# Context and output matmuls of an attention block as two 64-row tiles, ordered by a GpSimd relay

## The chip, the cores and the metric

One NeuronCore of one Trainium2 chip. The metric is the device time of the core in microseconds (us); lower is better. A ratio is the mean time of one kernel's runs over that of the other's of the same rounds, so it is not quite the ratio of the medians that are quoted.

## The reference

A layer norm, then two branches on the normalized rows: a sliding-window attention over a cache (32 heads of 192, the last 512 keys, 2048 query rows) and a SwiGLU feed-forward whose SiLU gates the attention output.

```
xn = layernorm(x)                                    # (1, 2048, 640)
q  = xn @ wq                                         # 32 heads of 192
s  = softmax(q k^T / sqrt(192)) v                    # last 512 keys of the cache
s  = s.reshape(2048, 32 * 192) @ wo                  # 640 columns
g  = silu((silu(xn @ w_gate) * (xn @ w_up)) @ w_down)
return x + s * g
```

## The kernel before

The kernel walks over 16 pairs of heads. A pair has two phases on TensorE. The first makes projections (`q_rows`) and scores for four blocks `b` of 512 rows; its matmuls use 64 of the array's 128 rows, two at a time (the "lo" and "hi" partitions). The second makes context (`pv`, N = 193) and output projection (`wo_tile`, N = 320); its matmuls use all 128 rows. The output lags the context by two blocks, since the context is transposed by a DMA in between. PSUM is two tags of two buffers each: `sc` (scores and output tiles) and `mm` (projections and context). Buffers of a tag are taken in turn.

```python
    def sc_tile():
        return psum.tile([P, 2, 512], f32, name="sc", tag="sc")     # bufs=2
    def mm_tile():
        return psum.tile([P, 2, 512], f32, name="mm", tag="mm")     # bufs=2
...
    def scores(i, kc):
        khat, qT, ks = pairs[i // NB]["khat"], qTs[i], slice(kc * P, (kc + 1) * P)
        sc = mm_tile() if i == NS - 1 and kc < 2 else sc_tile()
        for j in range(3):
            for h, r in enumerate((lo, hi)):
                nc.tensor.matmul(
                    sc[:, h, :], khat[r, j, ks], qT[r, j, :], start=(j == 0), stop=(j == 2)
                )
        p_t = ppool.tile([P, 2, 512], bf, name="p_t")
        nc.scalar.activation(p_t[:, :, :], sc[:, :, :], ACT.Exp, scale=scale)
...
    def pv(i, q2):
        ...
        acc = sc_tile() if alone and q2 and b < 2 else mm_tile()
        for k in range(2):
            qt = 2 * q2 + k
            for h in range(2):
                for kc in range(KC):
                    nc.tensor.matmul(
                        acc[:, k, h * 256 : h * 256 + Dh + 1],
                        Ps[i][kc][:, h, qt * P : (qt + 1) * P], V_p[:, kc, h, 0 : Dh + 1],
                        start=(kc == 0), stop=(kc == KC - 1),
                    )
        ...                      # reciprocal on VectorE, four scaled copies on ScalarE to O_b
        if pr == last or i == 0:
            ...                  # a transposing DMA for each half of the block
        elif pr < last and q2 == 1:
            nc.sync.dma_start_transpose(
                out=OT_b[:, :, :], in_=O_b[:, :, :, :].rearrange("p t h d -> p (t h d)")
            )
...
        for b in range(NB):
            i = pr * NB + b
            for q2 in range(2):
                pv(i, q2)
                if i >= 2:
                    wo_tile(i - 2, 2 * q2)
                    wo_tile(i - 2, 2 * q2 + 1)
```

The softmax here doesn't subtract the row's maximum and nothing guards it: scores larger than these inputs give would overflow.

Of the kernel before, what the change touches and what calls it, by code (L numbers as in the profile page):

```python
# [10 lines left out]
ALU = mybir.AluOpType  # L11
# [4 lines left out]
def kernel(  # L16
# [13 lines left out]
    nc = tc.nc  # L30
    P = nc.NUM_PARTITIONS
# [4 lines left out]
    _, Hkv, Sk, Dh = A_k_cache.shape  # L36
# [8 lines left out]
    NB = Sq // 512  # L45
    KC = W // P
# [4 lines left out]
    HD = D // 2  # L51
    scale = float(Dh) ** -0.5
    EPS = 1e-5
    bf = dt.bfloat16
    f32 = dt.float32
# [6 lines left out]
    kk, vv, wq, wo = A_k_cache[0], A_v_cache[0], A_wq, A_wo  # L62
# [8 lines left out]
    def sc_tile():  # L71
        return psum.tile([P, 2, 512], f32, name="sc", tag="sc")

    def mm_tile():
        return psum.tile([P, 2, 512], f32, name="mm", tag="mm")
# [5 lines left out]
    g2 = res.tile([P, T, D], bf, name="g2")  # L81
# [11 lines left out]
    V_p = consts.tile([P, KC, 2, Dh + 2], bf, name="V_p")  # L93


    pairs = {}
# [46 lines left out]
    def sum_k(pr, c):  # L143
        d = pairs[pr]
        nc.vector.reduce_sum(d["ssum"][:, c : c + 1], d["KT"][:, c, :], axis=AX.X)

    lo, hi = slice(0, 64), slice(64, 128)
# [17 lines left out]
    with ExitStack() as fctx:  # L165
# [154 lines left out]
        first = {f: [sc[:, s, :] for s in range(2)] for f, sc in ((0, sc_tile()), (1, sc_tile()))}  # L320
# [16 lines left out]
        banks = [(f, s) for f in range(3) for s in range(2)]  # L337
# [69 lines left out]
    opool = ctx.enter_context(tc.tile_pool(name="att_o", bufs=2))  # L407
    otpool = ctx.enter_context(tc.tile_pool(name="att_ot", bufs=3))
    smpool = ctx.enter_context(tc.tile_pool(name="att_sm", bufs=8))
    finp = ctx.enter_context(tc.tile_pool(name="fin", bufs=2))  # L410
    sacc = sapool.tile([P, T, D], f32, name="sacc")

    NS = NPAIR * NB
    last = NPAIR - 1
    Ps, OTs, Obs, xrs = {}, {}, {}, {}

# [3 lines left out]
    def q_rows(i, j):  # L420
        pr, b = divmod(i, NB)
        if j == 0:
            qTs[i] = qpool.tile([P, 3, 512], bf, name="qT")
        q_ps = mm_tile()
        for c in range(NC):
            for h, r in enumerate((lo, hi)):
                nc.tensor.matmul(  # L427
                    q_ps[:, h, :], pairs[pr]["wq"][r, c, j * P : (j + 1) * P], xnT[r, c, b * 512 : (b + 1) * 512],
                    start=(c == 0), stop=(c == NC - 1),
                )  # L430
        with nc.allow_low_precision(reason="a sum of two, rounded once, like a copy out of PSUM"):
            nc.vector.reduce_sum(  # L432
                qTs[i][:, j, :], q_ps[:, :, :].rearrange("p h n -> p n h"), axis=AX.X
# [6 lines that stand above are left out]
# [8 lines left out]
    def pv(i, q2):  # L448

        pr, b = divmod(i, NB)  # L450
        if q2 == 0:
            Obs[i] = opool.tile([P, 4, 2, Dh], bf, name="O_b")
            tag = "OT_l" if late(i) and pr < last else "OT_b"
            OTs[i] = otpool.tile([P, 12, P], bf, name=tag, tag=tag, bufs=2 if tag == "OT_l" else 3)
        O_b, OT_b = Obs[i], OTs[i]
        alone = i < 2 or (pr == last and 2 * b + q2 < 5)
        acc = sc_tile() if alone and q2 and b < 2 else mm_tile()
        r = smpool.tile([P, 2, 2, 1], f32, name="r")
        for k in range(2):
            qt = 2 * q2 + k  # L460
            for h in range(2):
                for kc in range(KC):
                    nc.tensor.matmul(  # L463
                        acc[:, k, h * 256 : h * 256 + Dh + 1],
                        Ps[i][kc][:, h, qt * P : (qt + 1) * P], V_p[:, kc, h, 0 : Dh + 1],
                        start=(kc == 0), stop=(kc == KC - 1),
                    )
        a_v = acc[:, :, :].rearrange("p k (h c) -> p k h c", h=2)
        nc.vector.reciprocal(r[:], a_v[:, :, :, Dh : Dh + 1])  # L469
        for k in range(2):  # L470
            qt = 2 * q2 + k
            a_k = a_v[:, k, :, :]
            if k == 0 and alone:
                nc.vector.tensor_tensor(  # L474
                    O_b[:, qt, :, :], a_k[:, :, 0:Dh], r[:, k, :, :].to_broadcast([P, 2, Dh]),
                    ALU.mult,
                )
                continue
            for h in range(2):
                nc.scalar.activation(  # L480
                    O_b[:, qt, h, :], a_k[:, h, 0:Dh], ACT.Copy, scale=r[:, k, h, :]
                )
        if pr == last or i == 0:
            nc.sync.dma_start_transpose(
                out=OT_b[:, 6 * q2 : 6 * q2 + 6, :],
                in_=O_b[:, 2 * q2 : 2 * q2 + 2, :, :].rearrange("p t h d -> p (t h d)"),
            )
        elif pr < last and q2 == 1:
            nc.sync.dma_start_transpose(
                out=OT_b[:, :, :], in_=O_b[:, :, :, :].rearrange("p t h d -> p (t h d)")  # L490
            )

    def load_xr(t):
        xrs[t] = finp.tile([P, D], bf, name="x_r", bufs=8)
        nc.sync.dma_start(out=xrs[t][:], in_=x2[t * P : (t + 1) * P, :])


    def late(i):
        return i // NB >= NPAIR - 2 and i % NB >= 2

    def wo_mm(ps, i, qt, n, first=True, end=True):
        for j in range(3):
            nc.tensor.matmul(  # L503
                ps, OTs[i][:, 3 * qt + j, :], pairs[i // NB]["wo"][:, j, n * HD : (n + 1) * HD],
                start=(first and j == 0), stop=(end and j == 2),
            )

    def wo_tile(i, qt):
        pr, b = divmod(i, NB)
        t = 4 * b + qt  # L510
        sc = sc_tile()
        for n in range(2):
            wo_mm(sc[:, n, 0:HD], i, qt, n)
        s_t = sacc[:, t, :].rearrange("p (n d) -> p n d", n=2)
        if pr == 0:
            nc.vector.tensor_copy(out=s_t, in_=sc[:, :, 0:HD])
        else:
            nc.vector.tensor_tensor(s_t, s_t, sc[:, :, 0:HD], ALU.add)  # L518

        if pr == last - 1 or late(i + NB):  # L520
            nc.gpsimd.tensor_tensor(sacc[:, t, :], sacc[:, t, :], g2[:, t, :], ALU.mult)  # L521
            if pr < last - 1:
                add_x(t)

    def add_x(t):
        nc.gpsimd.tensor_tensor(sacc[:, t, :], sacc[:, t, :], xrs[t][:], ALU.add)
# [29 lines left out]
    def store(left):  # L556
        while len(stores) > left:
            t, ob = stores.pop(0)
            nc.sync.dma_start(out=out2[t * P : (t + 1) * P, :], in_=ob[:])

    for pr in range(NPAIR):
        for b in range(NB):
            i = pr * NB + b
            for kc in range(KC):
                if kc < 3 and i + 1 < NS:
                    q_rows(i + 1, kc)
                scores(i, kc)
                if pr < last:
                    if b == 0:
                        transpose_k(pr + 1, kc)  # L570
                    elif b == 2 and kc < 3:
                        sum_k(pr + 1, kc)
                    elif b == 3:
                        centre_k(pr + 1, kc)
                        if kc == 3:
                            centre_k(pr + 1, 4)
            if b == 0:
                load_v(pr)
                if pr >= last - 1:
                    for t in range(8):  # L580
                        load_xr(t + 8 if pr < last else t)
                        if pr == last:
                            add_x(t)
        if pr == last:
            break
        for b in range(NB):
            i = pr * NB + b
            for q2 in range(2):
                pv(i, q2)
                if i >= 2:  # L590
                    wo_tile(i - 2, 2 * q2)
                    wo_tile(i - 2, 2 * q2 + 1)
            if b == 0 and pr + 2 < NPAIR:
                load_k(pr + 2)
            elif b == 1 and pr + 2 < NPAIR:
                load_wq(pr + 2)
            elif b == 2:
                load_wo(pr + 1)
    i = last * NB
    V, G = nc.vector, nc.gpsimd  # L600
    work = [(0, 0), (0, 1), (1, 0), (1, 1), (2, 0)]
    for b, q2 in work:
        pv(i + b, q2)
    for b, q2, more in ((0, 0, (2, 1)), (0, 1, (3, 0)), (1, 0, (3, 1)), (1, 1, None)):
        for k in range(2):
            wo_last(b, 2 * q2 + k, G)
        if more:
            pv(i + more[0], more[1])
    for b in (2, 3):
        for qt in range(4):  # L610
            store(0 if (b, qt) == (3, 3) else 3)
# [31 lines left out]
```

## Time and profile before

| | before |
|---|---|
| device time, median | 927.87 us (927.74 to 927.89, 4 runs) |
| profiled span | 925.9 us |
| TensorE busy | 918.9 us, 99% |
| one pair, start to start | 47.24 us: 23.42 projections and scores, 23.83 context and output |
| mode changes of TensorE in pairs 0-13 | 28, each 0.096 us over the normal spacing |

TensorE is the bound, so the total is read off its start times: what is late there is late at the end. The useful view is the order of time around the two borders of a pair, since the start of a group, less that of the group before, against the number of matmuls in it, shows what was lost between them. The lines are in the prediction.

### The profile page before, as it was taken

The numbers are of one execution on the slowest core, as the hardware profiler recorded it, in microseconds if no ns is written. First come the engines' busy times: TensorE is split into PE (matmuls) and PEld (weight loads), VectorE is DVE, ScalarE is ACT, GpSimd is POOL, SyncE is SP. The second block draws the span as 40 slices with busy tenths as digits, with TensorE's granted clock in tenths as the row PEclk, the third lists the DMA queues.
The fourth block names the chain that finished last, engine by engine and source line by source line (L and its number), as shares of the span: only waits on it lengthen the run. The fifth ranks groups of instructions, "written<-read, shape, count | busy, mean of one in ns | idle before, by whom it ended". The sixth has DMA issues, their size and how long they took to land. (4 is left out here: it accounts for less than half of the span.)

```text
span 925.9 us, 18772 instructions
## 1 busy us (share of the span) xinstructions
PE 918.9 (99%) x7997; PEld 578.0 (62%) x8013; DVE 576.6 (62%) x844; ACT 474.0 (51%) x847; POOL 68.0 (7%) x59
## 2 busy tenths in 40 slices
PE   9999999999999999999999999999999999999997
PEld 5455556574848474757575757565666666666665
DVE  6433331467676767676666667676767676767655
ACT  4222222556465656565555555555555565656561
POOL 0000000000000000000000000000000000002977
PEclk9999999999999999999999999999999999999999
DMA  9321510053525343343434252526262616162524
GB/s 296 74 53 35 114 35 1 1 93 71 101 63 92 73 85 79 76 88 70 94 68 96 59 106 55 109 49 116 40 124 35 129 35 125 37 132 75 142 50 140
DMA packets 241892, 76.73 MB, mean 83 GB/s; under 512 B 222736, under 2 KB 241808, under 8 KB 241808
## 3 DMA queue, kind: packets, MB, share of 16 engines
q1 hardware_dynamic: 240752, 74.71, 38.1%
q8 instruction: 63, 1.03, 0.5%
q10 hardware_dynamic: 1056, 0.82, 0.3%
q14 instruction: 21, 0.17, 0.1%
HBM read 39.45 MB, written 2.62 MB: 45 GB/s over the span
## 5 line engine op out<-in xcount | busy, mean ns | idle before, releaser
L445 ACT ACTIVATE p_t<-sc 128x1024 bf16<-128x1024 f32 x254 | 253.0, 1022 | 136.6 <-PE sc L441 136.6
L432 DVE TENSOR_REDUCE qT<-mm 128x512 bf16<-128x1024 f32 x189 | 231.3, 1224 | 104.0 <-PE mm L427 101.6
L480 ACT ACTIVATE O_b<-mm,r 128x192 bf16<-128x192 f32 x486 | 164.7, 421 | 176.5 <-DVE r L469 96.6
L427 PE MATMUL mm<-xnT,wq_p 64*128 64x512 bf16 x1890 | 235.1, 377 | 0.0
L503 PE MATMUL sc<-wo_p,OT_b 128*128 128x320 bf16 x1482 | 223.1, 299 | 0.0
L518 DVE TENSOR_TENSOR sacc<-sacc,sc 128x640 f32<-128x640 f32 x216 | 176.7, 821 | 60.9 <-PE sc L503 60.9
L441 PE MATMUL sc<-qT,khat 64*128 64x512 bf16 x1524 | 195.6, 376 | 0.0
L463 PE MATMUL mm<-V_p,p_t 128*128 128x193 bf16 x1984 | 186.0, 246 | 0.0
L463 PEld LDWEIGHTS <-p_t 128*128 128x128 bf16 x2048 | 173.0, 97 | 15.0 <-issue 7.0
L503 PEld LDWEIGHTS <-OT_b 128*128 128x128 bf16 x1488 | 143.4, 97 | 47.6
L427 PEld LDWEIGHTS <-wq_p 64*128 64x128 bf16 x1890 | 90.8, 94 | 112.3 <-issue 4.2
L441 PEld LDWEIGHTS <-khat 64*128 64x128 bf16 x1536 | 74.8, 94 | 91.0
L284 DVE TENSOR_TENSOR hT<-sc,sg 128x512 bf16<-128x512 f32 x46 | 31.7, 690 | 85.2 <-ACT sg L283 85.1
L521 POOL TENSOR_TENSOR sacc<-sacc,g_76 128x640 f32<-128x640 f32 x16 | 22.1, 1401 | 757.8 <-ACT O_b L480 757.8
L469 DVE RECIPROCAL r<-mm 128x4 f32<-128x4 f32 x124 | 22.7, 183 | 73.2 <-PE mm L463 69.0
L283 ACT ACTIVATE sg<-sc 128x512 bf16<-128x512 f32 x46 | 27.3, 596 | 72.4 <-PE sc L276 72.4
L276 PE MATMUL sc<-xnT,wg_sb 128*128 128x512 bf16 (+1 forms) x248 | 58.6, 354 | 0.6
L276 PE MATMUL sc<-xnT,wu_sb 128*128 128x512 bf16 (+1 forms) x259 | 59.0, 355 | 0.1
L298 PE MATMUL mm<-wd_sb,hT 128*128 128x320 bf16 x384 | 56.6, 299 | 0.0
L298 PEld LDWEIGHTS <-hT 128*128 128x128 bf16 x384 | 37.5, 98 | 19.0
L276 PEld LDWEIGHTS <-wu_sb 128*128 128x128 bf16 x285 | 26.3, 98 | 27.0 <-DMA wu_sb<-in_B_w_up_dram 0.3
L276 PEld LDWEIGHTS <-wg_sb 128*128 128x128 bf16 x285 | 26.4, 98 | 23.1
(60 smaller groups left out, 247.0 us busy)
## 6 DMA issues: line engine op xcount, KB each, us to landing
wo_p<-in_A_wo_dram SPq DMA_DIRECT2D x16, 480.0 KB, 4.3
K_p<-in_A_k_cache_dram SPq DMA_DIRECT2D x32, 192.0 KB, 3.2
V_p<-in_A_v_cache_dram SPq DMA_DIRECT2D x32, 192.0 KB, 3.1
wq_p<-in_A_wq_dram SPq DMA_DIRECT2D x64, 80.0 KB, 3.1
wq_p<-in_A_wq_dram SPq DMA_DIRECT2D x16, 160.0 KB, 3.3
x_r<-in_A_x_dram SPq DMA_DIRECT2D x16, 160.0 KB, 3.8
x_t<-in_A_x_dram SPq DMA_DIRECT2D x14, 160.0 KB, 3.5
wd_sb<-in_B_w_down_dram SPq DMA_DIRECT2D x1, 1920.0 KB, 12.1
```

What stands on the lines that cost most here:

```text
L276: nc.tensor.matmul(out, w_sb[:, c, f * P : (f + 1) * P], xnT[:, c, qc], start=(c == 0), stop=(c == NC - 1),)
L283: nc.scalar.activation(sg[:], g, ACT.Silu)
L284: nc.vector.tensor_tensor(hTs[b][:, f, :], u, sg[:], ALU.mult)
L298: nc.tensor.matmul(dn[:, 0:HD], hTs[b][:, f, ti * P : (ti + 1) * P], wd_sb[:, f, cols], start=(f == 0), stop=(f == NF - 1),)
L427: nc.tensor.matmul(q_ps[:, h, :], pairs[pr]["wq"][r, c, j * P : (j + 1) * P], xnT[r, c, b * 512 : (b + 1) * 512], start=(c == 0), stop=(c ...
L432: nc.vector.reduce_sum(qTs[i][:, j, :], q_ps[:, :, :].rearrange("p h n -> p n h"), axis=AX.X)
L441: nc.tensor.matmul(sc[:, h, :], khat[r, j, ks], qT[r, j, :], start=(j == 0), stop=(j == 2))
L445: nc.scalar.activation(p_t[:, :, :], sc[:, :, :], ACT.Exp, scale=scale)
L463: nc.tensor.matmul(acc[:, k, h * 256 : h * 256 + Dh + 1], Ps[i][kc][:, h, qt * P : (qt + 1) * P], V_p[:, kc, h, 0 : Dh + 1], start=(kc == ...
L480: nc.scalar.activation(O_b[:, qt, h, :], a_k[:, h, 0:Dh], ACT.Copy, scale=r[:, k, h, :])
L503: nc.tensor.matmul(ps, OTs[i][:, 3 * qt + j, :], pairs[i // NB]["wo"][:, j, n * HD : (n + 1) * HD], start=(first and j == 0), stop=(end an ...
L518: nc.vector.tensor_tensor(s_t, s_t, sc[:, :, 0:HD], ALU.add)
```

## The change

Each context and output matmul of pairs 0-13 is cut into two of 64 rows, so TensorE never leaves the 64-row mode in these pairs. (Below, a "drain" is the loss of 0.096 us at a mode change, and a "couple" is a lo and a hi matmul that start together.) Two row tiles must not write one PSUM bank at the same time (Gotcha 1 of the skill's page on tiling, as the prediction cites it). So lo writes bank 0 while hi writes bank 1 (first half), then they swap banks and accumulate (second half). The swap has to wait for the first half's writes, so a tiny GpSimd memset is put in as a relay, which waits for one half and is waited for by the other: last matmul of half 1, memset, first matmul of half 2. To keep TensorE busy meanwhile, one context tile `x` and two output tiles `y`, `z` are woven. In pair 14 and 15 the old code stays (`pv_full`, `wo_full`). The core of the diff:

```diff
+    turn_t = smpool.tile([P, 1], f32, name="turn_t", bufs=1)
...
+        def part(p):                                   # of pv: p = 0..3
...
+            turn, h = divmod(p, 2)
+            for kc in range(KC):
+                for n, r in enumerate((lo, hi)):
+                    k = n ^ turn
+                    qt = 2 * q2 + k
+                    m = nc.tensor.matmul(
+                        acc[:, k, h * 256 : h * 256 + Dh + 1],
+                        Ps[i][kc][r, h, qt * P : (qt + 1) * P], V_p[r, kc, h, 0 : Dh + 1],
+                        start=(p == 0 and kc == 0), stop=(turn == 1 and kc == KC - 1),
+                        skip_group_check=True,
+                    )
+                    after(m, st)
+            if p == 1:
+                turned(m, st)
...
+    def turned(m, st):
+        st["turn"] = nc.gpsimd.memset(turn_t[:], 0.0)
+        follows(st["turn"], m)
+
+    def after(m, st):
+        if "turn" in st:
+            follows(m, st.pop("turn"))
...
+    def two(x, y):
+        for part in (*x[:2], *y[:2], *x[2:], *y[2:]):
+            part()
+
+    def woven(x, y, z):
+        for part in (y[0], *x[:2], y[1], z[0], *x[2:], z[1]):
+            part()
...
-            for q2 in range(2):
-                pv(i, q2)
-                if i >= 2:
-                    wo_tile(i - 2, 2 * q2)
-                    wo_tile(i - 2, 2 * q2 + 1)
+            if i < 2:
+                two(pv(i, 0), pv(i, 1))
+            else:
+                for q2 in range(2):
+                    if pr < last - 1:
+                        woven(pv(i, q2), wo_tile(i - 2, 2 * q2), wo_tile(i - 2, 2 * q2 + 1))
+                    else:
+                        pv_full(i, q2)
+                        wo_full(i - 2, 2 * q2)
+                        wo_full(i - 2, 2 * q2 + 1)
```

More of the change, by code (lines that the diff above doesn't have):

```diff
@@ L450, in pv, with divide @@
         pr, b = divmod(i, NB)
-        if q2 == 0:
-            Obs[i] = opool.tile([P, 4, 2, Dh], bf, name="O_b")
-            tag = "OT_l" if late(i) and pr < last else "OT_b"
-            OTs[i] = otpool.tile([P, 12, P], bf, name=tag, tag=tag, bufs=2 if tag == "OT_l" else 3)
+        st = {}
+        def part(p):
+            if p == 0:
+                if q2 == 0:
+                    Obs[i] = opool.tile([P, 4, 2, Dh], bf, name="O_b")
+                    tag = "OT_l" if late(i) and pr < last else "OT_b"
+                    OTs[i] = otpool.tile([P, 12, P], bf, name=tag, tag=tag, bufs=2 if tag == "OT_l" else 3)
+                st["alone"] = i < 2 or (pr == last and 2 * b + q2 < 5)
+                st["acc"] = sc_tile() if st["alone"] and q2 and b < 2 else mm_tile()
+            acc = st["acc"]
+            turn, h = divmod(p, 2)
[12 more added lines that the diff above has]
+                turned(m, st)
+            if p == 3:
+                divide(i, q2, acc, st["alone"])
+        return [lambda p=p: part(p) for p in range(4)]
+    def divide(i, q2, acc, alone):
+        pr, b = divmod(i, NB)
         O_b, OT_b = Obs[i], OTs[i]
-        alone = i < 2 or (pr == last and 2 * b + q2 < 5)
-        acc = sc_tile() if alone and q2 and b < 2 else mm_tile()
         r = smpool.tile([P, 2, 2, 1], f32, name="r")
-        for k in range(2):
-            qt = 2 * q2 + k
-            for h in range(2):
-                for kc in range(KC):
-                    nc.tensor.matmul(
-                        acc[:, k, h * 256 : h * 256 + Dh + 1],
-                        Ps[i][kc][:, h, qt * P : (qt + 1) * P], V_p[:, kc, h, 0 : Dh + 1],
-                        start=(kc == 0), stop=(kc == KC - 1),
-                    )
         a_v = acc[:, :, :].rearrange("p k (h c) -> p k h c", h=2)
@@ L491, in pv, with pv_full @@
             )
+    def pv_full(i, q2):
+        pr, b = divmod(i, NB)
+        if q2 == 0:
+            Obs[i] = opool.tile([P, 4, 2, Dh], bf, name="O_b")
+            tag = "OT_l" if late(i) and pr < last else "OT_b"
+            OTs[i] = otpool.tile([P, 12, P], bf, name=tag, tag=tag, bufs=2 if tag == "OT_l" else 3)
+        O_b, OT_b = Obs[i], OTs[i]
+        alone = i < 2 or (pr == last and 2 * b + q2 < 5)
+        acc = sc_tile() if alone and q2 and b < 2 else mm_tile()
+        for k in range(2):
+            qt = 2 * q2 + k
+            for h in range(2):
+                for kc in range(KC):
+                    nc.tensor.matmul(
+                        acc[:, k, h * 256 : h * 256 + Dh + 1],
+                        Ps[i][kc][:, h, qt * P : (qt + 1) * P], V_p[:, kc, h, 0 : Dh + 1],
+                        start=(kc == 0), stop=(kc == KC - 1),
+                    )
+        divide(i, q2, acc, alone)
     def load_xr(t):
@@ L506, in wo_mm, with follows, wo_turn, first @@
             )
-    def wo_tile(i, qt):
+    def follows(m, earlier):
+        tc.add_manual_dep(
+            m.ins, earlier.ins.name,
+            mybir.DependencyInfo(mybir.DependencyClass.Sync, mybir.DependencyReason.DATA),
+            reason="row tiles change banks",
+        )
+    def turned(m, st):
[4 more added lines that the diff above has]
+            follows(m, st.pop("turn"))
+    def wo_turn(st, i, qt, turn):
+        ps = st["sc"]
+        for j in range(3):
+            for k, r in enumerate((lo, hi)):
+                n = k ^ turn
+                m = nc.tensor.matmul(
+                    ps[:, n, 0:HD], OTs[i][r, 3 * qt + j, :], pairs[i // NB]["wo"][r, j, n * HD : (n + 1) * HD],
+                    start=(turn == 0 and j == 0), stop=(turn == 1 and j == 2), skip_group_check=True,
+                )
+                after(m, st)
+        if turn == 0:
+            turned(m, st)
+    def wo_tile(i, qt):
+        pr, b = divmod(i, NB)
+        t = 4 * b + qt
+        st = {}
+        def first():
+            st["sc"] = sc_tile()
+            wo_turn(st, i, qt, 0)
+        def second():
+            sc = st["sc"]
+            wo_turn(st, i, qt, 1)
+            s_t = sacc[:, t, :].rearrange("p (n d) -> p n d", n=2)
+            if pr == 0:
+                nc.vector.tensor_copy(out=s_t, in_=sc[:, :, 0:HD])
+            else:
+                nc.vector.tensor_tensor(s_t, s_t, sc[:, :, 0:HD], ALU.add)
+            if pr == last - 1 or late(i + NB):
+                nc.gpsimd.tensor_tensor(sacc[:, t, :], sacc[:, t, :], g2[:, t, :], ALU.mult)
+                if pr < last - 1:
+                    add_x(t)
+        return [first, second]
+    def wo_full(i, qt):
         pr, b = divmod(i, NB)
@@ L587 @@
             i = pr * NB + b
-            for q2 in range(2):
-                pv(i, q2)
-                if i >= 2:
-                    wo_tile(i - 2, 2 * q2)
-                    wo_tile(i - 2, 2 * q2 + 1)
+            if i < 2:
+                two(pv(i, 0), pv(i, 1))
+            else:
+                for q2 in range(2):
+                    if pr < last - 1:
+                        woven(pv(i, q2), wo_tile(i - 2, 2 * q2), wo_tile(i - 2, 2 * q2 + 1))
+                    else:
+                        pv_full(i, q2)
+                        wo_full(i - 2, 2 * q2)
+                        wo_full(i - 2, 2 * q2 + 1)
             if b == 0 and pr + 2 < NPAIR:
@@ L602 @@
     for b, q2 in work:
-        pv(i + b, q2)
+        pv_full(i + b, q2)
     for b, q2, more in ((0, 0, (2, 1)), (0, 1, (3, 0)), (1, 0, (3, 1)), (1, 1, None)):
@@ L607 @@
         if more:
-            pv(i + more[0], more[1])
+            pv_full(i + more[0], more[1])
     for b in (2, 3):
```

## The prediction

> **What bounds the kernel now.** I read the page first: busy shares, then the costliest groups, then the table of stretches for the attention part, and last the order of time around the two places where TensorE changes between 64-row and 128-row matmuls.
>
> From the page (busy us, share, count), and two stretches of the table (us and count for PE, PEld, DVE, ACT, POOL, then clock, DMA share, GB/s):
>
> ```profile
> PE 918.9 (99%) x7997; PEld 578.0 (62%) x8013; DVE 576.6 (62%) x844; ACT 474.0 (51%) x847; POOL 68.0 (7%) x59
> ...
> 300.00:400.00 100.00, 100.00 (x933) 64.44 (x933) 69.34 (x96) 55.65 (x103) 0.00 (x0) 1.00 0.40 84
> 515.60:539.40 23.80, 23.80 (x226) 19.98 (x224) 14.70 (x27) 12.09 (x34) 0.00 (x0) 1.00 0.55 109
> ```
>
> TensorE is never idle in the pair loop, at full granted clock; VectorE and ScalarE have a third or more of their time free and GpSimd does nothing there. A busy TensorE can still lose time inside, since its spans overlap, so I went to the order of time. First the change from scores (64-row) to context and output (128-row) matmuls of one pair, then the change back:
>
> ```profile
> 514.24 1.46 PE L441 MATMUL sc<-qT,khat 64*128 64x512 bf16 x12
> 514.45 1.23 DVE L432 TENSOR_REDUCE qT<-mm 128x512 bf16<-128x1024 f32 x1
> 515.09 1.94 ACT L445 ACTIVATE p_t<-sc 128x1024 bf16<-128x1024 f32 x2 [0.70 <-PE sc L441]
> 515.63 1.28 PEld L463 LDWEIGHTS <-p_t 128*128 128x128 bf16 x16 [0.42 <-issue]
> 515.63 1.51 PE L463 MATMUL mm<-V_p,p_t 128*128 128x193 bf16 x16
> ...
> 516.98 1.79 PE L503 MATMUL sc<-wo_p,OT_b 128*128 128x320 bf16 x12
> 517.25 0.18 DVE L469 RECIPROCAL r<-mm 128x4 f32<-128x4 f32 x1 [0.46 <-PE mm L463]
> 517.51 1.35 ACT L480 ACTIVATE O_b<-mm,r 128x192 bf16<-128x192 f32 x4 [0.48 <-ACT p_t L445]
> 517.99 1.64 DVE L518 TENSOR_TENSOR sacc<-sacc,sc 128x640 f32<-128x640 f32 x2 [0.56 <-PE sc L503]
> 518.47 1.40 PEld L463 LDWEIGHTS <-p_t 128*128 128x128 bf16 x16
> 518.61 1.50 PE L463 MATMUL mm<-V_p,p_t 128*128 128x193 bf16 x16
> ```
>
> ```profile
> 537.73 1.79 PE L503 MATMUL sc<-wo_p,OT_b 128*128 128x320 bf16 x12
> ...
> 539.45 0.76 PEld L427 LDWEIGHTS <-wq_p 64*128 64x128 bf16 x10 [0.26 <-issue]
> 539.46 1.25 PE L427 MATMUL mm<-xnT,wq_p 64*128 64x512 bf16 x10
> ...
> 541.19 1.24 PE L427 MATMUL mm<-xnT,wq_p 64*128 64x512 bf16 x10
> ...
> 542.27 0.81 PE L441 MATMUL sc<-qT,khat 64*128 64x512 bf16 x6
> ```
>
> Starts give the real rates. 10 matmuls from 541.19 to 542.27 are five couples of 64-row tiles at 0.216 us; 16 context matmuls from 515.63 to 516.98 take 0.084 us each (median start to start 83 ns); 12 output matmuls from 516.98 to 518.61 take 0.136 each. The mode changes show as excess: 12 score matmuls should take 6 x 0.216 = 1.296 us, but 515.63 - 514.24 is 1.39; 12 output matmuls should take 1.632, but 539.46 - 537.73 is 1.73. Each change costs 0.096 us (in all pairs 0.307 to 0.309 between starts instead of 0.212, and 0.231 to 0.232 instead of 0.136). A pair takes 47.24 us (successive context phases start at 515.63 and 562.87), so the two changes are 0.19 us of it: 0.4%, all that the change's intent can win.
>
> **What the Trainium skill says.** "TensorEngine Tiling (Array Packing)", Tiling Modes, Key Properties: "Changing tiling mode (not just tile) drains the TensorE". The trace agrees, at 0.096 us each way. The same page, Restrictions and Gotchas, Gotcha 1: different row tiles may not access the same PSUM bank simultaneously, and software must synchronize them. That is why each half writes crossed banks and a relay separates the halves; no wait of this kind is in the trace yet. "TensorE: Matmul & The Clock Gate", Back-to-back issue gap, gives N/2.4 + 2.5 ns: 82.9, 135.8 and 215.8 for N = 193, 320, 512; the trace has 83, 136 and 216, and 216 for a couple of 64-row tiles too. So a couple costs what one full-height matmul of that N costs, at least for N = 512. The same page, part 1 (on the 56 ns gap), says start to start never falls under about 25 ns however small N is; the trace has nothing so short except the second matmul of a couple, 4 ns behind the first.
>
> **The change part by part.** A woven unit of new work is: output half A1, context halves 1 (both heads), A2, B1, context halves 2, B2. The arithmetic is the same: 16 couples of N = 193 in place of 16 matmuls, 12 couples of N = 320 in place of 12. At 83 and 136 ns a couple the unit keeps 16 x 0.083 + 12 x 0.136 = 2.96 us, which is 518.61 - 515.63 = 2.98 before. Eight units a pair.
>
> (1) Removed: two mode changes in each of pairs 0-13, 28 x 0.096 = 2.7 us. It is on the bounding engine, so it counts in full.
>
> (2) Added, the relay: last matmul of a half, GpSimd memset of 128x1, first matmul of the next half. Estimate of its latency from the trace: a matmul's start to end 0.246 (N = 193) or 0.299 (N = 320); another engine's end to GpSimd's start about 0.08 to 0.09 (VectorE to rstd); such a memset 0.10 (the ones at the start); to a waiting matmul 0.05 (as VectorE to an output matmul at 908.14). Sum 0.48 after a context half, 0.53 after an output half. The gap that other work fills, last start to dependent start: after an output half 0.132 + 8 x 0.083 = 0.80; after the context half 0.08 + 6 x 0.136 = 0.90. Spare 0.27 and 0.42 us, so the relay lies hidden: 0. GpSimd has 24 a pair of 0.1 us, one per us, and no other work in these pairs.
>
> (3) Moved: in pairs 1-13 the first matmul of the context phase is now output half A1, into an "sc" buffer, where a context matmul into an "mm" buffer stood. There are two sc buffers. The last two score tiles of the phase were issued back to back (the x12 above), and A1 gets the buffer of the first of them, free only when its exponential is done: the first of the two in the 515.09 line, which ends at 516.12. With 0.05 for the semaphore A1 starts at 516.17. Before, context began at 515.63 (515.54 without the drain). The old order hid that exponential behind 1.33 us of context work; the new one doesn't. Loss against before: 516.17 - 515.63 = +0.54 us, in which the drain saved there is already counted.
>
> (4) Moved: context of the last unit ends closer to the phase's end E, at E - 0.41 rather than E - 1.63. Its mm buffer is wanted by the second projection of the next phase, at E + 1.08 + 0.65 = E + 1.73. Its last matmul starts at E - 0.49; from there to the end of the four ScalarE divisions was 1.97 us before (516.895 to 518.87), so E + 1.48. It fits, with 0.2 to spare. The sc buffer of A lives 1.48 us + 0.2 + VectorE's 0.82, about 2.6 with the semaphore, and is wanted after 2.96; B likewise. No wait.
>
> Sum: pairs 1-13, +0.54 - 0.096 = +0.44 each, 5.8 us; pair 0 starts with context tiles alone and wins 0.19. +5.6 us: 927.9 becomes about 933.5.
>
> **The rivals.**
> (A) The couple of N = 193 does not keep 83 ns. It needs four TensorE instructions (two weight loads, two matmuls) in 83 ns, 21 each. The fastest sustained stretch of the trace has two in 54 to 56 (the transposes, 27 each). For: that rate is unproved, and the skill's 25 ns floor, if it held for each instruction, would make a couple 100 ns: 17 ns x 128 couples x 14 pairs = 30 us, 958. Against: in the projection the two tiles' weight loads start 2 to 4 ns apart and both take 94 ns, as one alone does, so they run side by side; and full-height loads of 97 ns are already hidden at 83 and even 55 ns. I give a clear slowdown of this kind about one chance in five, with 940 to 960.
> (B) The wait of (3) is not there, for instance since the buffers fall the other way. Then only the drains are won: 925.2. Against: buffers are taken in turn, 16 score tiles and 16 output tiles a pair, both even; and ScalarE begins that exponential at once after its scores, so nothing earlier can free it. About one in eight.
> (C) The relay is longer than its spare. 0.1 us too much on each of 24 x 13 would add 31 us; the memsets of the trace wait for nothing, so their latency behind a matmul is my estimate. Spare of half its length speaks against. One in twelve.
>
> **Range and chances.** Centre 933.5 with two thirds of the weight within 931 to 937; below it (B) at 925, above it (A) and (C) spread from 938 to 965. A range of 925 to 948 leaves about 5% below and 15% above. Faster by over 2% means under 909, which 2.7 us of possible gain excludes: 0.01. Slower by over 2% is above 946.4: 0.16. The same within 2%: 0.83.
>
> **What would show it.** Step 1: excess between starts at the changes of phase falls from 0.096 to 0 at the way back, with no wait. Step 3: some 13 new waits of TensorE for ScalarE's exponential, about 0.6 us each, before the first output matmul of a pair; if the chain of waits has none, (3) is wrong. Step 2: no TensorE wait for GpSimd; GpSimd shows some 330 short memsets. Rates: context couples at 83 ns and output couples at 136; if couples of N = 193 stand further apart in a unit with no wait, (A) is the cause. Step 4: no wait of the second projection for ScalarE.

## The result, and the profile after

The changed kernel takes 938.92 us (938.79 to 939.75, 4 runs) against 927.87: ratio 1.0121, interval 1.0106 to 1.0135. That is 11.05 us slower: inside the range, and on the slow side of the sign, but twice the 5.6 us of the central sum.

First, in the same pair as before, the border from scores to the second phase (order of time of the changed kernel: start, duration, engine, line, operation, count, and in brackets the idle time ahead with what ended it):

```profile
519.68 1.47 PE L442 MATMUL sc<-qT,khat 64*128 64x512 bf16 x12
...
520.54 1.94 ACT L446 ACTIVATE p_t<-sc 128x1024 bf16<-128x1024 f32 x2 [0.70 <-PE sc L442]
...
521.62 0.58 PE L568 MATMUL sc<-wo_p,OT_b 64*128 64x320 bf16 x6 [0.46 <-ACT p_t L446]
521.62 0.24 PEld L568 LDWEIGHTS <-OT_b 64*128 64x128 bf16 x5 [0.77 <-issue]
521.89 0.75 PEld L468 LDWEIGHTS <-p_t 64*128 64x128 bf16 x16
522.02 0.85 PE L468 MATMUL mm<-V_p,p_t 64*128 64x193 bf16 x16
522.32 0.10 POOL L556 MEMSET turn_t<- 128x1 f32 x1 [25.34 <-PE sc L568]
522.61 0.74 PEld L568 LDWEIGHTS <-OT_b 64*128 64x128 bf16 x12
522.69 0.99 PE L568 MATMUL sc<-wo_p,OT_b 64*128 64x320 bf16 x12
```

From the twelve score matmuls to the first output matmul it is 521.62 - 519.68 = 1.94 us, where 1.30 would do and 1.39 stood before. The first output matmul waited for an exponential of ScalarE. The bracket shows 0.46, not 0.64, because the profile counts a matmul as busy until its modelled end. After that the weave runs without a gap: 8 couples of N = 193 from 522.02 to 522.69 are 0.67 us (83 ns a couple), and the 12 matmuls (6 couples of N = 320) between 522.69 and the next context group, at 523.50 in the same view, take 0.81 (136 ns a couple). The relay memset starts at 522.32, ends at 522.42, and its matmul starts at 522.69, 0.27 us later (how much of it is to spare is measured below, with relay_384). No line of the waits has TensorE waiting for GpSimd.

Next, a place that I had not foreseen. In pair 8 (again in order of time):

```profile
576.69 1.30 SPq L507 DMA_TRANSPOSE OT_b<-O_b  x1
...
580.74 0.59 PE L568 MATMUL sc<-wo_p,OT_b 64*128 64x320 bf16 x6
...
582.05 0.25 PEld L568 LDWEIGHTS <-OT_b 64*128 64x128 bf16 x6 [1.07 <-DMA OT_b<-O_b]
582.06 0.58 PE L568 MATMUL sc<-wo_p,OT_b 64*128 64x320 bf16 x6 [0.73 <-DMA OT_b<-O_b]
```

A half of an output tile needs 0.41 us, so the second group was due at 581.15 and came at 582.06. It waited for the transposing DMA that SyncE issued at 576.69 and that landed 5.32 us later.

How much room such a transpose has shows in an earlier pair. Its issue, and the group that holds its first reader, before the change (order of time):

```profile
521.81 1.44 SPq L489 DMA_TRANSPOSE OT_b<-O_b  x1
...
528.84 1.79 PE L503 MATMUL sc<-wo_p,OT_b 128*128 128x320 bf16 x12
```

and after it:

```profile
529.02 1.44 SPq L507 DMA_TRANSPOSE OT_b<-O_b  x1
...
533.07 0.99 PE L568 MATMUL sc<-wo_p,OT_b 64*128 64x320 bf16 x12
```

The last group is two halves of 0.41 us, of which the second, at 533.48, is the first reader. The room was 7.0 us and is 4.5.

The whole list of such waits of TensorE in the changed kernel (who waited for whom: us in total, times, longest):

```profile
PEld L568 <- issue: 9.9, 13, 0.8
...
PEld L568 <- DMA OT_b<-O_b: 6.7, 7, 1.4
...
PE sc L568 <- ACT p_t L446: 6.0, 13, 0.5
...
PE sc L568 <- DMA OT_b<-O_b: 3.6, 5, 1.2
```

Before the change this table has no such line for the output matmuls in these pairs. The first and third line are the weight load and the matmul of one event a pair, thirteen times: pairs 1 to 13. The DMA lines likewise overlap; by start times there are seven events. One of them is put down to a VectorE add (0.9 us) and was the DMA: its transpose landed at 342.74 and the matmul started at 342.79.

The starts of the score phases split the 11.1 us by pair. An undisturbed pair takes 47.67 us after the change against 47.24 before, +0.427, and there are 13 of them: 5.55 us. The first pair takes 42.70 against 40.72, +1.98. Five later stretches show 1.05, 0.93, 0.61, 0.11 and 1.01 us on top, 3.7 together; all but the 0.11 (a second projection that started 0.11 late, at 644.05) are waits for the transposing DMA. That is 5.55 + 1.98 + 3.70 - 0.14 (an earlier start of the first score phase) = 11.09: the last common start, the scores of pair 15, is at 882.33 against 871.24.

Why are some transposes late? The page of each kernel counts what the instruction fetch moves (queue, kind: packets, MB, share of the DMA engines). Before:

```profile
q8 instruction: 63, 1.03, 0.5%
```

After:

```profile
q8 instruction: 87, 1.43, 0.6%
```

The matmuls and weight loads of these phases are twice as many, and this queue moved 24 more packets of 16 KB. In the DMA records of nine traces (all but the one with halved transposes) I took every context transpose of over 3 us and asked whether an instruction packet was in flight during it. Without one, 176 landed within 4.6 us and 1 did not; with one, 241 did and 105 did not. A longer transpose has more time to meet a packet; but counting only packets in flight within its first 3.7 us, the usual time of a whole transpose, gives the same four numbers. The kernel's own loads do not separate them: beside a load in the first 3 us 101 of 496 were slow, without one 5 of 27. The slow ones exist before the change as well (7 of 57). They cost nothing there: the longest took 5.6 us, and the room was 7.0.

### The profile page after: what moved, and what is told of

It reads as the page before. It is cut to its first block, busy times and chain, and to the rows that moved or that the text cites. A ratio compares the mean times of both kernels' runs of the same rounds, so it can differ in the third digit from the quotient of the medians.

```text
span 936.9 us, 25618 instructions
## 1 busy us (share of the span) xinstructions
PE 920.3 (98%) x11101; PEld 613.0 (65%) x11101; DVE 576.7 (62%) x844; ACT 474.5 (51%) x847; POOL 100.2 (11%) x387
## 4 chain that ended last, share of the span: by engine, by line
PE 94%; DMA 3%; ACT 2%; DVE 1%; issue 0%; SPq 0%; DVEq 0%
PE mm L428 22%; PE sc L568 18%; PE sc L442 17%; PE mm L468 14%; PE sc L276 11%; PE mm L298 6%; PE sc L542 3%; DMA OT_b<-O_b 3%; PE mm L525 2%; ACT p_t L446 1%; PE sc L219 1%; PE mm L276 0%; PE mm L311 0%; PE sc L525 0%; ACT O_b L498 0%
## 5 line engine op out<-in xcount | busy, mean ns | idle before, releaser
L568 PE MATMUL sc<-wo_p,OT_b 64*128 64x320 bf16 x2592 | 217.5, 296 | 10.6 <-ACT p_t L446 6.0
L593 DVE TENSOR_TENSOR sacc<-sacc,sc 128x640 f32<-128x640 f32 x200 | 164.2, 821 | 89.7 <-PE sc L568 89.7
L468 PE MATMUL mm<-V_p,p_t 64*128 64x193 bf16 x3520 | 185.7, 242 | 0.0
L468 PEld LDWEIGHTS <-p_t 64*128 64x128 bf16 x3584 | 161.4, 93 | 11.2
L428 PEld LDWEIGHTS <-wq_p 64*128 64x128 bf16 x1890 | 101.4, 94 | 100.4 <-issue 0.8
L568 PEld LDWEIGHTS <-OT_b 64*128 64x128 bf16 x2592 | 135.9, 94 | 39.0 <-issue 9.9
L442 PEld LDWEIGHTS <-khat 64*128 64x128 bf16 x1536 | 82.4, 94 | 83.3
L556 POOL MEMSET turn_t<- 128x1 f32 x328 | 32.2, 98 | 709.4 <-PE sc L568 544.4
```

The costliest lines, as they stand in the source:

```text
L428: nc.tensor.matmul(q_ps[:, h, :], pairs[pr]["wq"][r, c, j * P : (j + 1) * P], xnT[r, c, b * 512 : (b + 1) * 512], start=(c == 0), stop=(c ...
L442: nc.tensor.matmul(sc[:, h, :], khat[r, j, ks], qT[r, j, :], start=(j == 0), stop=(j == 2))
L468: m = nc.tensor.matmul(acc[:, k, h * 256 : h * 256 + Dh + 1], Ps[i][kc][r, h, qt * P : (qt + 1) * P], V_p[r, kc, h, 0 : Dh + 1], start=(p ...
L556: st["turn"] = nc.gpsimd.memset(turn_t[:], 0.0)
L568: m = nc.tensor.matmul(ps[:, n, 0:HD], OTs[i][r, 3 * qt + j, :], pairs[i // NB]["wo"][r, j, n * HD : (n + 1) * HD], start=(turn == 0 and j ...
L593: nc.vector.tensor_tensor(s_t, s_t, sc[:, :, 0:HD], ALU.add)
```

## The experiments

Two theories were put against each other. Theory 1: row tiles and relay are free, and the loss is order, in two parts: (1a) the first output tile of a phase takes an `sc` buffer that an exponential still reads, (1b) context is transposed later and wanted earlier. Theory 2: row tiles or relay cost the time themselves. All eight kernels gave correct results.

### order_alone: the old matmuls in the new kind of order

```diff
-                        woven(pv(i, q2), wo_tile(i - 2, 2 * q2), wo_tile(i - 2, 2 * q2 + 1))
+                        wo_full(i - 2, 2 * q2)
+                        pv_full(i, q2)
+                        wo_full(i - 2, 2 * q2 + 1)
...
-                two(pv(i, 0), pv(i, 1))
+                pv_full(i, 0)
+                pv_full(i, 1)
```

> Full-height matmuls, no relay, both mode changes kept; only the order in pairs 0-13 is the new one in spirit: output tile A, context, output tile B, where before it was context, A, B. Theory 1 (the loss is order: the first output tile of a phase waits for an exponential to free its score buffer, and the output wants its transposed context earlier): the first output matmul of pairs 1-13 starts about 0.54 us later than context did before (13 x 0.54 = 7.0 us), plus 1 to 2 us of waits for the transposing DMA, so 935 to 938 us. Theory 2 (row tiles or the relay themselves cost the time): as before, 928 us.

Measured: 937.81 us, ratio to before 1.0106 (1.0092 to 1.012). No row tile and no relay, and still most of the loss. At the border of the same pair (order of time):

```profile
520.03 1.46 PE L442 MATMUL sc<-qT,khat 64*128 64x512 bf16 x12
...
520.88 1.94 ACT L446 ACTIVATE p_t<-sc 128x1024 bf16<-128x1024 f32 x2 [0.70 <-PE sc L442]
521.42 0.10 PEld L542 LDWEIGHTS <-OT_b 128*128 128x128 bf16 x1 [0.42 <-issue]
...
521.96 0.97 PE L542 MATMUL sc<-wo_p,OT_b 128*128 128x320 bf16 x6 [0.47 <-ACT p_t L446]
```

The weights were loaded at 521.42, as the mode change allows, and the matmul then stood until 521.96, when the first of the two exponentials (half of 1.94 us) was done. 521.42 is 1.39 after the scores' start, which is where the context matmuls stood before the change, so the loss is 0.54 us; the traces of this kernel and of before put each such border 0.53 or 0.54 apart, in 13 pairs 7.0 us. Four pairs and pair 0 have waits for the transposing DMA besides, 0.4 to 0.7 us each. Theory 2 falls as a main cause. In this profiled execution the feed-forward part began 0.9 us late behind a weight load, so the split is read from the pairs and not from the total.

### first_in_mm: the changed kernel with a free buffer at the border

```diff
-            st["sc"] = sc_tile()
+            st["sc"] = mm_tile() if (b, qt) == (2, 0) else sc_tile()
```

> The changed kernel, but the first output tile of each context phase in pairs 1-13 is put into an mm buffer, which is free, in place of the sc buffer that an exponential still reads. Theory 1: the 13 waits of 0.63 us vanish, 8.2 us less than the changed kernel: about 930.7 us; the waits for the transposing DMA (some 6 us in sum) stay, give or take 2. Theory 2 (row tiles or relay): no change, 938.9 us, the time shows up elsewhere.

Measured: 930.72 us (930.38 to 932.46), ratio to before 1.0033 (1.002 to 1.0047). Against the changed kernel 8.2 us are gone, which is 13 times 0.63. At the border (order of time):

```profile
517.43 1.46 PE L442 MATMUL sc<-qT,khat 64*128 64x512 bf16 x12
...
518.72 0.57 PE L568 MATMUL mm<-wo_p,OT_b 64*128 64x320 bf16 x6
```

518.72 - 517.43 = 1.29 us: no wait and no drain. Part (1a) is shown. An undisturbed pair takes 47.03 us in this trace, 0.21 less than before the change, so what is left over before is what waits for the DMA. (The profiled execution is the slowest of the four, 932.46 us, and its waits for the DMA are longer than those of the changed kernel's trace.)

### half_transposes: the changed kernel with a transpose for every unit

```diff
-        if pr == last or i == 0:
+        if pr != last - 1:
             nc.sync.dma_start_transpose(
```

> The changed kernel, but the context of every unit in pairs 0-13 is transposed by its own DMA (the first half one unit earlier, the second in about 2.8 us as in pair 0, not 3.7 to 5.5). Theory 1b (about 5.8 us of the loss are output matmuls waiting for a transposing DMA whose deadline the new order moved 2.6 us closer): the four waits of pairs 3, 8, 9 and 13 (3.6 us) vanish and pair 0 keeps 1.3 to 2.1: 934 to 935.5 us. Rival: the DMA queue is the limit, twice the transposes make the waits more: 939 us or over.

Measured: 935.15 us (934.61 to 935.63), ratio to before 1.0075 (1.006 to 1.0091). 3.8 us are gone; the predicted four waits were 3.6. One DMA wait is left in its trace, at 199.13 us in pair 0, as said. Part (1b) is shown for the later pairs, since nothing but the time at which the transposed context lands was altered. More DMA issues did no harm.

### relay_128 and relay_384: a longer relay

```diff
-    turn_t = smpool.tile([P, 1], f32, name="turn_t", bufs=1)
+    turn_t = smpool.tile([P, 128], f32, name="turn_t", bufs=1)       # relay_384: [P, 384]
```

> The changed kernel with a relay memset of 128x128 instead of 128x1, an estimated 0.2 us instead of 0.1. The trace of the changed kernel leaves 0.268 us between the memset's end and the matmul that it releases after an output half, 0.415 after a context half, of which some 0.05 is the semaphore. If the relay is hidden with that spare, 0.1 us more changes nothing: 938.9 us. If the relay is already part of the loss, 24 x 13 x 0.1 = 31 us more.

> The same with a memset of 128x384, an estimated 0.4 to 0.5 us. That is 0.1 to 0.2 us over the spare of 0.22 after output halves (16 a pair, 14 pairs, less in pair 0), and at most just over that of 0.37 after context halves: 15 to 50 us more than 938.9, with TensorE waits for GpSimd in the trace. No change would say that the relay is not what orders the halves.

Measured: 939.32 us (938.75 to 939.83) with 128, the same as the changed kernel; 958.12 (958.0 to 958.95) with 384, ratio to before 1.033 (1.0316 to 1.0344). The memset group of each trace (count, busy us, mean ns, idle before):

```profile
L556 POOL MEMSET turn_t<- 128x128 f32 x328 | 67.5, 206 | 673.9 <-PE sc L568 520.9 <-PE mm L468 152.1 <-PE sc L468 1.0
```

```profile
L556 POOL MEMSET turn_t<- 128x384 f32 x328 | 137.1, 418 | 623.9 <-PE sc L568 494.3 <-PE mm L468 129.1 <-PE sc L468 0.6
```

and in the waits of the second a line that no other woven kernel has at this size:

```profile
PEld L568 <- POOL turn_t L556: 34.6, 216, 0.2
```

0.206 us instead of 0.098 is free, 0.418 is not. The 216 waits are those after an output half (8 units of 2 in 13 pairs, 4 units in pair 0). Context halves of one unit start at 536.59 and 538.18 there, so a unit went from 2.96 to 2 x 1.59 = 3.18 us: 0.11 a wait. A memset that is 0.32 longer and loses 0.11 had 0.21 in hand; I had estimated 0.27. The relay does order the halves, and at its real length it lies hidden.

### rotated: the weave turned by one step

```diff
-                        woven(pv(i, q2), wo_tile(i - 2, 2 * q2), wo_tile(i - 2, 2 * q2 + 1))
+                if b == (2 if pr == 0 else 0):
+                    x = pv(i, 0)
+                    run(x[:2])
+                for q2 in range(2):
+                    y, z = wo_tile(i - 2, 2 * q2), wo_tile(i - 2, 2 * q2 + 1)
+                    run((y[0], *x[2:]))
+                    if (b, q2) == (NB - 1, 1):
+                        run((z[0], y[1], z[1]))
+                    else:
+                        x = pv(i + q2, 1 - q2)
+                        run((y[1], z[0], *x[:2], z[1]))
```

(`OTs[i]` is now allocated with the first `divide`, since half z of the old block still reads its buffer before that.)

> The changed kernel with the weave turned by one step: context halves 1 first in a phase, then in each unit A1, context halves 2, A2, B1, the next unit's context halves 1, B2. The first output tile comes 0.66 us after the phase's start, and context is done 1.5 us earlier against its output, so neither the exponential nor the DMA should be waited for. Theory 1: only the removed drains are left (2.7 us), less 1.3 to 2.1 us of pair 0's DMA wait and up to 0.1 us of relay wait a pair: 925.5 to 928 us. Theory 2 (row tiles or relay cost time): 933 us or more.

Measured: 928.04 us (5 runs), ratio to before 1.0001 (0.9989 to 1.0014); a hair over the expected 925.5 to 928. Both waits are gone in pairs 1-13 although row tiles and relay are all there. What remains is in three lines of its waits:

```profile
PEld L568 <- POOL turn_t L556: 2.8, 14, 0.2
PEld L466 <- POOL turn_t L556: 2.7, 13, 0.2
...
PEld L568 <- DMA OT_b<-O_b: 1.9, 2, 1.1
```

There are two relay waits a pair, one in the first unit (L466, context) and one in the last (L568, output), where only one output half stands between the two halves of a tile. In start times they are about 0.04 and 0.05 us, which is why a pair takes 47.14 us and not 47.05. And there are two DMA waits in pair 0 (0.65 and 0.95 us in start times).

### rotated_but_first and rotated_filled

The first leaves pair 0 in full-height matmuls. The second also puts context halves 1 of the first unit ahead of the last score tile, and the last output half behind the next phase's first projection.

```diff
-                two(pv(i, 0), pv(i, 1))
-            elif pr < last - 1:
+                pv_full(i, 0)
+                pv_full(i, 1)
+            elif 0 < pr < last - 1:
...                                        # rotated_filled alone:
+                run(held)
+                held.clear()
+                if 0 < pr < last - 1 and (b, kc) == (NB - 1, KC - 1):
+                    early.append(pv(pr * NB, 0))
+                    run(early[0][:2])
                 scores(i, kc)
...
-                        run((z[0], y[1], z[1]))
+                        run((y[1], z[0]))
+                        held.append(z[1])
```

> The turned weave, but pair 0 stays in full-height matmuls as before the change, since its waits for the transposing DMA (0.65 and 0.95 us) were all that the turned weave still lost there. Theory 1: pairs 1-13 win the 2 x 0.1 us of drains, less some 0.1 us of relay wait a pair that the turned weave showed: 927.9 - 13 x 0.1 = 926.5 us, 926 to 927.

> The same, with the two short relay gaps of a phase filled: context halves 1 of the first unit go ahead of the phase's last score tile, and the last output half goes behind the next phase's first projection. Theory 1: both drains are won in full in pairs 1-13, 26 x 0.096 = 2.5 us: 925.4 us (925 to 926). Theory 2 (row tiles cost something of their own): not under 926.5.

Measured: 926.24 us, ratio to before 0.9985 (0.9973 to 0.9998), as expected; and 925.77 us (925.63 to 926.2), ratio 0.998 (0.9967 to 0.9994), within the expected 925 to 926. Its pairs take 47.11 us against 47.24, 0.13 of the possible 0.19. What is missing is in the order of time of the next phase's start:

```profile
540.30 0.81 DVE L593 TENSOR_TENSOR sacc<-sacc,sc 128x640 f32<-128x640 f32 x1
...
541.16 0.82 PE L442 MATMUL sc<-qT,khat 64*128 64x512 bf16 x6
```

The output half held back leaves its `sc` buffer only when VectorE's add is done at 541.11, and the second score tile starts at 541.16, 0.07 late. This kernel is the fastest of all, by 2.0 us over before, and it is the measure of what the idea was worth: 0.2%.

## Why the prediction was right, and where its sum was short

The signs and the steps came out as foretold, but the sum was half of what was measured. That 938.9 us lies in the range is in part luck: it is outside the central 931 to 937, and the room above was made for rivals (A) and (C), of which neither came true. A term that the prediction did not have filled it.

- **Part 1, the drains.** Right. With nothing else in the way a border costs 1.29 us where it cost 1.39 (first_in_mm), and the way back lost its 0.10 in every pair of the changed kernel.
- **Part 2, the relay.** Right in its verdict. The spare was 0.21 us after an output half and not 0.27, and twice the memset is still free. Rival (C) is out.
- **Rates, rival (A).** Out: couples run at 83 and 136 ns in the changed kernel, four TensorE instructions in 83 ns.
- **Part 3, the exponential.** Right in size and place: thirteen waits, 0.43 us net a pair against 0.44 predicted. Removing that wait alone (first_in_mm) took 8.2 us off. Rival (B) is out.
- **Part 4, the buffers at the phase's end.** Right but for one place: the second projection came late once in 14 borders, by 0.11 us.
- **What the sum left out.** Part 4 followed the PSUM buffers of the moved tiles and stopped there. It did not follow the transposed context, which leaves the core's engines for a DMA and comes back. The room of a transpose fell from 7.0 us to 4.5: counted from the start of the phase, context is transposed 1.2 us later and read 1.3 us earlier. A usual transpose takes 3.7 us and still fits; one of 5 to 5.5 us does not. This is the term that was missing: 2.2 us in pair 0 (+1.98, where -0.19 was predicted) and 3.6 of the 3.7 in the later pairs, together 5.8, where the sum was short by 5.5. The difference is the 0.11 of the late projection, less 0.2 by which part 3 was too high and less the 0.14 of an earlier start. half_transposes took 3.8 of them away, and turning the weave with pair 0 left alone took away all.
- **Open.** That an instruction packet in flight makes a transpose slow is an association in the DMA records (105 of 346 slow with one, 1 of 177 without). That a longer transpose meets more packets does not explain it (the count within the first 3.7 us is the same). But no run took the packets away, so it is not shown as a cause.

## What to carry to other kernels

When a change only reorders work on the bounding engine, list for every moved piece both what it needs and what needs it, and include the trips that leave the engines, such as a transposing DMA: a deadline of 7 us had room for the slow tail, one of 4.5 us had room for the usual 3.7 but not for the tail. At a border of two phases that share a PSUM tag, the first user of the tag waits for the last reader of the other phase; start with work of the other tag. And size the prize first: two drains of 0.1 us in 47 us can't pay for one wait of 0.6.

## What the Trainium skill lacked or had wrong

- "TensorEngine Tiling (Array Packing)", Tiling Modes, Key Properties, says that a change of mode drains TensorE but gives no size. Here it is 0.096 us each way (0.308 us instead of 0.212 between starts, and 0.232 instead of 0.136).
- The same page, Gotcha 1, leaves the synchronization of row tiles to software and names no means or price. Here a GpSimd memset of 128x1 between two halves costs 0.098 us by itself and is hidden behind 0.66 us of other matmuls, with 0.21 us in hand; a memset of 0.418 us there costs 0.11 each time.
- "TensorE: Matmul & The Clock Gate", on the 56 ns gap, has a floor of about 25 ns from start to start. It does not hold between matmuls of different row tiles, for which the same page, part 3, has about 4 ns: here the second of a couple starts 4 ns (before) or 20 ns (median, after) behind the first. What the page lacks is the rate of couples with an N well under 512: couples of N = 193 follow each other at 83 ns, with two weight loads and two matmuls in each.
- "Runtime: NRT & Kernel Launch", Instruction fetch mechanics, has the fetch in blocks of 16 KiB on a DMA queue of its own, and the packets here are of 16 KB: 63 before and 87 after on one queue. What I found on no page is whether it slows a kernel's own transfers: of the transposes that overlapped an instruction packet 30% took over 4.6 us (usual 3.7, slowest 6.3), of the others 1 in 177. Whether the packet is the cause stays open.
